# Attention and Fourier mixing on one core: normalisation moved from VectorE to ScalarE in six more batches, and folds dealt in five pieces

## The chip, the core and the metric

The kernel runs on one core of a Trainium2 chip. The metric is the device time of one execution in microseconds (us), as the median of several runs; lower is better. A core has five engines with a queue each: TensorE (PE; its weight loads are listed apart as PEld), VectorE (DVE), ScalarE (ACT), GpSimd (POOL) and SyncE (SP), which here only issues DMAs. [...]

## What is computed

Eight batches, eight heads, 576 tokens, 64 channels per head, all in float32. First comes attention in which each query keeps its 32 largest scores; then, on the 512 joined channels, the real part of a two-dimensional Fourier transform is added, and a normalised two-layer network on top of it.

```python
scores = scale * np.matmul(q, k.transpose(0, 1, 3, 2))
kth = np.partition(scores, -top_k, axis=-1)[..., -top_k:-top_k + 1]
scores = np.where(scores >= kth, scores, -1000000000.0)
attn = np.exp(scores - np.max(scores, axis=-1, keepdims=True))
attn = attn / (np.sum(attn, axis=-1, keepdims=True) + 1e-09)
attn_out = np.matmul(attn, v)                      # (B, H, S, D)
x = attn_out.transpose(0, 2, 1, 3).reshape(B, S, H * D)
u = x + np.real(np.fft.fft(np.fft.fft(x, axis=1), axis=2))
un = (u - u.mean(-1)) / np.sqrt(u.var(-1) + 1e-06)
out = u + np.maximum(un @ w_ch1, 0.0) @ w_ch2
```

## The kernel before

**Tiles and steps.** Two heads make a pair; a batch has four pairs (NPB), the kernel 32. A pair's scores are cut into nine tiles of 128 query rows by 576 keys, so there are 288 tiles (N), 36 per batch (PER_BATCH). The main loop (L1390) makes one step per tile, and a step i works on several tiles at once: it makes the scores of tile i+3, finds the largest values of tiles i and i+1, masks tile i-1, transposes the probabilities of tile i-2, and after the fifth and the ninth tile of a pair multiplies them with the values. Everything is written out by hand in the order of emission (`manual_schedule`, L1169); an engine runs its instructions in that order.

**The chain of a tile.** TensorE multiplies queries and keys (`scores`, L306; sp L368, tail keys sp_t L338), ScalarE copies the result to S (L371, L342, L360). VectorE takes four rounds of the eight largest values (L389) and three of striking them out (L391). GpSimd derives two bounds nt (`bounds`, L398). ScalarE and GpSimd mask the tile (`mask`, L405 and L408), ScalarE takes the exponential with its row sums (`expo`, L414). TensorE transposes the result (tpP, L435), ScalarE copies it to PT (L438), and `attend` (L463) multiplies it with the values into o (L472), in two parts per pair: ch 0 (three token blocks) and ch 1 (two). These parts are called half pairs below. `attended` copies o to xT (L486) and prepares the reciprocals rd of the row sums (L498, L499).

**From the half pair to x.** `to_tokens` (L502) turns xT back with TensorE into the tile tpx (L512) and multiplies each head's 64 columns by its reciprocal into x, which is [tokens, 512 channels] of the batch. Two ways of doing the multiplication are there: `normalise` on VectorE (L516, and L523 for the short block of ch 0), queued at the end of the same step's VectorE work (`late_now`), and `normalise_on_act` on ScalarE (L535, six multiplications of 64 columns for ch 0, four for ch 1), queued for the next step under "act". In the main loop "act" is run after the first fixed piece of TensorE's work and the mask of tile i-1 (L1450 to L1454). The second way is taken in batch 1 alone, but for its last half pair (L541).

tpx and o come from the PSUM pool ps_o, which has one buffer (L122), so a tile of either kind must have been read before the next is written; this holds from batch 1 on. In batch 0 tpx takes one of three other banks. x has two buffers; `to_tokens` of batch b waits, in the written-out order, until the output of batch b-2 has been sent (L1415 to L1421), and half pairs that had to wait follow each other in consecutive steps, save that from step 76 on none goes into the step of an attention product.

**Folds and transforms.** When x of a batch is complete, `fold_ops` (L607) makes sums and differences of it for each parity `par` of the token frequency: first (L627), second (L586), and third(n) for n = 0, 1, 2, which fold the channels (`fold_channels`, L556: n = 0 in L562 and L559, n = 1 in L559, L573 and L574, n = 2 in L559, L581 and L582). n = 0 writes what n = 1 reads; n = 1 writes columns 0 to 255 of the result fg (and takes one column of n = 0's), n = 2 columns 256 to 511. `dft_tokens` (L644) then reads columns 0 to 255 first and 256 to 511 second as weights of TensorE (yp, L663). In batches 1 to 6 the folds run on GpSimd in the steps named by `at(..., "pool0", ...)` (L1309, L1318), ahead of `bounds` (L1495, L1497); in batches 0 and 7 VectorE does them all in one step. The token DFT of a parity is placed at `ft`: steps T0 + 4 and T0 + 7 in batch 1, T0 + 5 and T0 + 11 in batches 2 to 6.

**The rest of TensorE's work.** The network of batch b-1 runs as `units` during batch b: hidden layer hp (L874, evicted by ScalarE L878), second layer cp, cv, cw (L901, L1071). A planner (`fixed_cost`, `level`, `some`, L1351 to L1385) spreads the units over the steps by estimated TensorE costs; the change touches none of these costs.

Of the kernel before, what the change touches and what calls it, by code (L numbers as in the profile page):

```python
# [72 lines left out]
def kernel(  # L73
# [21 lines left out]
    NPB = H // 2  # L95
# [33 lines left out]
    def bank(shape, name, hold=False):  # L129
        n = banks_free.pop(0)  # L130
        t = ps_m.tile(shape, F32, name=name, tag=f"m{n}", bufs=1)
        if not hold:
            banks_free.append(n)
            return t
        return t, lambda: banks_free.append(n)
# [366 lines left out]
    def to_tokens(pair, ch, at_once=True):  # L502

        b, hp = divmod(pair, NPB)
        if b not in x_of:
            x_of[b] = batp.tile([P, 5, DM], F32, name=f"x_{b}", tag="x", bufs=2)
        x = x_of[b]
        xT, rd = xT_of.pop((pair, ch)), rd_of.pop((pair, ch))
        shape, name = [P, 4, P], f"tpx_{pair}_{ch}"
        tp = ps_o.tile(shape, F32, name=name, tag="o") if at_once else bank(shape, name)  # L510
        for n, t in enumerate(CHUNKS[ch]):
            nc.tensor.transpose(tp[0:ROWS[t], n, :], xT[:, P * n:P * n + ROWS[t]], ident)  # L512
        cols = slice(P * hp, P * (hp + 1))

        def normalise():
            nc.vector.tensor_tensor(  # L516
                out=x[:, 2 * ch:2 * ch + 2, cols].rearrange("p t (e d) -> p t e d", e=2),
                in0=tp[:, 0:2, :].rearrange("p t (e d) -> p t e d", e=2),
                in1=rd[:, 0:4].rearrange("p (t e) -> p t e", e=2).to_broadcast([P, 2, 2, D]),
                op=ALU.mult,  # L520
            )
            if ch == 0:
                nc.vector.tensor_tensor(  # L523
                    out=x[0:TAIL, 4, cols].rearrange("p (e d) -> p e d", e=2),
                    in0=tp[0:TAIL, 2, :].rearrange("p (e d) -> p e d", e=2),
                    in1=rd[0:TAIL, 4:6].to_broadcast([TAIL, 2, D]),
                    op=ALU.mult,
                )

        def normalise_on_act():  # L530
            for n, t in enumerate(CHUNKS[ch]):
                r = slice(0, ROWS[t])
                for e in range(2):
                    hd = slice(D * e, D * (e + 1))
                    nc.scalar.mul(  # L535
                        out=x[r, t, cols][:, hd], in_=tp[r, n, hd],
                        mul=rd[r, 2 * n + e:2 * n + e + 1],
                    )


        if b == 1 and (hp, ch) != (NPB - 1, 1):  # L541
            at(now[0] + 1, "act", normalise_on_act)
        else:
            (late_now if at_once else late_next).append(normalise)
        return 0.14 * len(CHUNKS[ch])
# [38 lines left out]
    def fold_halves(eng, s_, z):  # L584
        for cols, op in ((slice(0, Q2), ALU.add), (slice(Q2, DM), ALU.subtract)):
            eng.tensor_tensor(out=z[..., cols], in0=s_[..., 0:Q2], in1=s_[..., Q2:DM], op=op)  # L586
# [20 lines left out]
    def fold_ops(b, par, eng, space="own"):  # L607

        x = x_of[b]

        if space == "hT":
            sp = batp.tile([P, NIT * CW[0]], F32, name=f"fsp_{b}", tag="hT")

        def buf(n, name, cols=DM):
            if space == "hT":
                return sp[:, 2 * DM * n:2 * DM * n + 2 * cols].rearrange("p (s c) -> p s c", s=2)
            pool, tag = (batp, ("fold_s", "fold_d")) if space == "own" else (attp, ("PT0", "PT1"))
            return pool.tile([P, 2, cols], F32, name=f"{name}_{b}_{par}", tag=tag[n % 2], bufs=1)  # L620

        got = folded[b, par] = []

        def first():
            got.append(buf(0, "sd"))
            op = ALU.add if par == 0 else ALU.subtract
            eng.tensor_tensor(out=got[0], in0=x[:, 0:2, :], in1=x[:, 2:4, :], op=op)  # L627

        def second():
            got.append(buf(1, "zw"))  # L630
            fold_halves(eng, got[0], got[1])

        def third(n):
            if n == 0:
                got.append(buf(2, "fg", DM + Q2))
            fold_channels(eng, got[1], got[2][:, :, 0:DM], got[2][:, :, DM:DM + Q2], n)

        def both():
            third(0)
            third(1)  # L640

        return [first, second, both, lambda: third(2)]

    def dft_tokens(b, par):  # L644
        for g2 in range(2):
            half_of_tokens(b, par, g2)
        return 4.3
# [96 lines left out]
    def add_mixed(b, t):  # L744
        rows, x = ROWS[t], x_of[b]
        us = us_of[b, t > 1 and t < 4][0:rows, CHUNKS[CHUNK_OF[t][0]].index(t), :]
        nc.gpsimd.tensor_tensor(out=x[0:rows, t, :], in0=x[0:rows, t, :], in1=us, op=ALU.add)
# [460 lines left out]
    def at(step, where, fn, cost=0.0):  # L1208
        plan.setdefault((step, where), []).append(fn)
        costs[step] = costs.get(step, 0.0) + cost  # L1210
# [75 lines left out]
    for b in range(B):  # L1286
        end = PER_BATCH * (b + 1) - 1
        last = b == B - 1
        first, soon = b == 0, b == 1
        T0 = end + (2 if first else 3 if soon else 4)  # L1290
        if first:

            for op in fold_tails(b, nc.gpsimd):
                at(T0 - 1, "pool", op)

            def folds(b=b):
                for par, space in ((0, "own"), (1, "hT")):
                    for op in fold_ops(b, par, nc.vector, space):
                        op()
            at(T0, "dve", folds)  # L1300
            ft, fc = (T0 + 1, T0 + 1), T0 + 1
        elif soon:

            for n, op in enumerate(fold_tails(b, nc.gpsimd)):
                at(T0 - 2 + n, "pool0", op)
            for par in range(2):
                def folds(par=par, b=b, T0=T0):
                    for n, op in enumerate(fold_ops(b, par, nc.gpsimd)):
                        at(T0 + 1 + 3 * par + min(n, 2), "pool0", op)  # L1309
                at(T0, "begin", folds)  # L1310
            ft, fc = (T0 + 4, T0 + 7), T0 + 8
        elif not last:
            for n, op in enumerate(fold_tails(b, nc.gpsimd)):
                at(T0 - 2 + n, "pool0", op)
            for par in range(2):
                def folds(par=par, b=b, T0=T0):
                    for n, op in enumerate(fold_ops(b, par, nc.gpsimd)):
                        at(T0 + (6 if par else 1) + n, "pool0", op)  # L1318
                at(T0, "begin", folds)
            ft, fc = (T0 + 5, T0 + 11), T0 + 12  # L1320
        else:
            for op in fold_tails(b, nc.gpsimd):
                at(T0 - 1, "pool0", op)

            def folds(b=b):
                for op in fold_ops(b, 0, nc.vector) + fold_ops(b, 1, nc.vector, "PT"):
                    op()
            at(T0, "dve", folds)

            at(T0 + 1, "pe1", lambda: one_unit() + one_unit() if len(queue) > 1 else 0.0)  # L1330
            ft, fc = (T0 + 1, T0 + 3), T0 + 4
        for par in range(2):
            at(ft[par], "pe1", lambda b=b, par=par: dft_tokens(b, par), 4.3)
        for n, t in enumerate((0, 1, 4, 2, 3)):
            quick = first or last
            s = fc + (0 if first else n // 3 if last else n // 2)
            at(s, "pe2", lambda b=b, t=t, q=quick: dft_channels(b, t, q), 1.75)
            if not quick:
                at(s, "pool2", lambda b=b, t=t: add_mixed(b, t))
                at(s + 1, "dve", lambda b=b, t=t: stats(b, t))  # L1340
            at(s + (1 if quick else 2), "pe", lambda b=b, t=t: channels_first(b, t), 0.6)
            if first and t == 4:
                at(s + 1, "pe", lambda: (queue.extend(waiting), waiting.clear()) and 0.0)
        at(s + 1, "begin" if quick else "dve", lambda b=b: rsqrt(b))
        arrivals.append(s + (1 if quick else 2))
        at(arrivals[-1], "units", lambda b=b: (queue if b else waiting).extend(mlp_units(b)))
# [28 lines left out]
    def one_unit():  # L1375
        c, fn, _ = queue.pop(0)
        fn()
        return c
# [11 lines left out]
    while i < N + 4 or plan or queue or sums:  # L1390
# [93 lines left out]
        first, second = top_ops(i, (2, 3)), top_ops(i + 1, (0, 1))  # L1484
# [62 lines left out]
```

## Time and profile before

| what | value |
|---|---|
| median of 3 runs | 1911.16 us (1910.43 to 1911.83) |
| the profiled execution | 1908.21 us, its span 1906.4 us |
| TensorE busy | 1789.7 us |
| VectorE busy | 1584.5 us |
| ScalarE busy | 1210.0 us |
| GpSimd busy | 909.8 us |
| normalise on VectorE, L516 | 57 times, 422 ns each |
| its second part, L523 | 28 times, 273 ns each |
| normalise on ScalarE, L535 | 36 instructions, 28 of them on 128 partitions (330 ns each) and 8 on 64 |
| folds on GpSimd: L627, L586, L559 (254 columns) | 2364, 1277 and 729 ns each |

A profile line of a group gives the line of the kernel, the engine, the operation, what is written and read, the shape and the count. A line of the waits gives who waited for whom, the sum in us, how often and the longest. A line of the timeline gives the start in us from the span's start, the length of the group in us, and in brackets the idle time before it and what ended that. Busy time of TensorE is that of pipelined matmuls whose ends are modelled.

### The profile page before, as it was taken

The page shows a single profiled execution, that of the slowest core. Times are in us where ns is not written, and L with a number is a line of the kernel's source. Part 1 is how long each engine was busy: PE and PEld are TensorE (multiplying, and loading weights), DVE is VectorE, ACT ScalarE, POOL GpSimd, SP SyncE. Part 2 cuts the span into 40 slices and gives each one's busy share as a digit, 9 for nine tenths or more (in the row PEclk, how much of TensorE's full clock was granted, in tenths as well). Part 3 has the DMA queues.
Part 4 walks back from the last instruction along what each step waited for, and adds up shares of the span by engine and source line. Part 5 has one row for each costly group of instructions (what it writes and reads, how often), then busy time and mean ns, then how long its engine had stood idle before and what let it go on. Part 6 is the DMA issues. An engine that isn't in the chain of part 4 may idle for free.

```text
span 1906.4 us, 28799 instructions
## 1 busy us (share of the span) xinstructions
PE 1789.7 (94%) x9200; PEld 1181.4 (62%) x9200; DVE 1584.5 (83%) x3301; ACT 1210.0 (63%) x3078; POOL 909.8 (48%) x1278
## 2 busy tenths in 40 slices
PE   6567799999999999999999999999999999999999
PEld 3344465474666756667567656667567656667677
DVE  8999999999999998889899988988899988872110
ACT  6878657676766767757676667666676667652100
POOL 4768643546635464345534464245534464241022
PEclk7778899999999999999999999999999999999999
DMA  5323002311104111130113101140113102030132
GB/s 165 112 86 108 20 13 57 92 55 25 47 7 130 33 25 47 42 108 27 25 47 101 50 20 53 41 114 22 25 47 100 51 19 57 25 103 6 50 105 75
DMA packets 184342, 111.25 MB, mean 58 GB/s; under 512 B 125952, under 2 KB 174208, under 8 KB 184192
## 3 DMA queue, kind: packets, MB, share of 16 engines
q1 hardware_dynamic: 183408, 109.20, 20.3%
q8 instruction: 74, 1.21, 0.3%
q14 instruction: 76, 0.62, 0.1%
q10 hardware_dynamic: 784, 0.21, 0.0%
HBM read 93.63 MB, written 15.73 MB: 57 GB/s over the span
## 4 chain that ended last, share of the span: by engine, by line
PE 74%; DVE 11%; ACT 6%; POOL 4%; issue 2%; DMA 2%; SPq 0%; POOLq 0%; DVEq 0%; ACTq 0%
PE hp L874 25%; PE cp L901 10%; PE o L472 7%; PE tpP L435 5%; PE sp L368 5%; DVE m L389 5%; PE cw L1071 5%; PE cv L1071 4%; DVE wk L391 4%; PE yp L663 3%; PE cp L940 3%; PE sp_t L338 2%; POOL wk L408 1%; ACT wk L414 1%; ACT wk L405 1%
## 5 line engine op out<-in xcount | busy, mean ns | idle before, releaser
L408 POOL TENSOR_TENSOR wk<-S,wk 128x576 f32<-128x576 f32 x288 | 408.9, 1420 | 730.8 <-ACT wk L405 697.3
L389 DVE MAX8 m<-wk 128x8 f32<-128x576 f32 x864 | 626.7, 750 | 6.1
L874 PE MATMUL hp<-unT,w 128*128 128x256 f32 (+1 forms) x2048 | 540.3, 411 | 2.6 <-ACT unT L792 2.6
L874 PEld LDWEIGHTS hp<-unT,w 128*128 128x128 f32 x2048 | 374.8, 191 | 124.8 <-issue 26.0
L391 DVE MATCH_REPLACE8 wk<-m,wk 128x576 f32<-128x576 f32 x576 | 427.7, 743 | 0.0
L414 ACT ACTIVATE wk<-wk,nt 128x576 f32<-128x576 f32 x288 | 225.0, 781 | 79.0 <-POOL wk L408 78.0
L405 ACT ACTIVATE wk<-S,nt 128x576 f32<-128x576 f32 x288 | 227.0, 788 | 34.1 <-POOL nt L398 32.9
L435 PE MATMUL tpP<-ident,wk 128*128 128x128 f32 x1152 | 183.4, 283 | 68.5 <-ACT wk L414 44.5
L901 PE MATMUL cp<-w,hT 128*128 128x512 f32 x512 | 240.6, 598 | 0.0
L438 ACT COPY PT<-tpP 128x512 f32<-128x512 f32 (+1 forms) x320 | 171.3, 547 | 106.2 <-PE tpP L435 103.8
L435 PEld LDWEIGHTS tpP<-ident,wk 128*128 128x128 f32 x1152 | 140.4, 145 | 143.7 <-ACT wk L414 67.9
L878 ACT ACTIVATE hT<-hp 128x320 f32<-128x320 f32 (+1 forms) x256 | 105.0, 410 | 195.2 <-PE hp L874 193.0
L389 DVE MAX8 m<-S 128x8 f32<-128x576 f32 x288 | 213.9, 743 | 6.8 <-ACT S L342 6.8
L391 DVE MATCH_REPLACE8 wk<-m,S 128x576 f32<-128x576 f32 x288 | 213.8, 742 | 0.0
L472 PE MATMUL o<-PT,v 128*64 128x256 f32 (+3 forms) x1440 | 193.3, 411 | 2.0 <-ACT PT L438 1.9
L371 ACT COPY S<-sp 128x512 f32<-128x512 f32 (+1 forms) x264 | 141.8, 588 | 50.7 <-PE sp L368 50.3
L368 PE MATMUL sp<-kT,qT 64*128 64x512 f32 (+1 forms) x528 | 161.2, 669 | 5.0 <-ACT means L1259 3.3
L472 PEld LDWEIGHTS o<-PT,v 128*64 128x64 f32 x1440 | 110.6, 151 | 72.8 <-issue 15.7
L901 PEld LDWEIGHTS cp<-w,hT 128*128 128x128 f32 x512 | 88.8, 190 | 86.3 <-issue 86.2
L1016 POOL TENSOR_TENSOR hT<-hT 128x512 f32<-128x512 f32 x64 | 81.5, 1276 | 100.1 <-ACT hT L878 88.4
L1071 PE MATMUL cw<-w,hT 128*128 128x256 f32 x448 | 106.7, 383 | 1.9 <-POOL nt L398 1.2
L1071 PEld LDWEIGHTS cw<-w,hT 128*128 128x128 f32 x448 | 81.4, 190 | 19.4 <-issue 5.2
(157 smaller groups left out, 2178.8 us busy)
## 6 DMA issues: line engine op xcount, KB each, us to landing
w<-w_parts SPq DMA_DIRECT2D x82, 512.0 KB, 4.5
space<-in_moe_w_ch_dram SPq DMA_DIRECT2D x32, 512.0 KB, 3.4
nat<-in_q_dram SPq DMA_DIRECT2D x128, 64.0 KB, 2.2
v<-in_v_dram SPq DMA_DIRECT2D x128, 64.0 KB, 2.2
out_dram<-x SPq DMA_DIRECT2D x32, 256.0 KB, 2.1
nat<-in_k_dram SPq DMA_DIRECT2D x124, 64.0 KB, 2.2
w_parts<-w_t SPq DMA_DIRECT2D x8, 512.0 KB, 2.9
w_s<-w_parts SPq DMA_DIRECT2D x8, 512.0 KB, 5.0
```

Of the source, the lines that this page charges most:

```text
L368: nc.tensor.matmul(sp[r], lhsT=qT[hd, q_cols], rhs=kT[hd, :], start=True, stop=True)
L389: ops.append(lambda src=src, m8=m8: nc.vector.max(out=m8, in_=src))
L391: ops.append(lambda src=src, m8=m8: nc.vector.match_replace(w, m8, src, NEG))
L405: nc.scalar.activation(out=w, in_=Ssb[i], func=AF.Relu, scale=-FAR, bias=Nt[i][:, 1:2])
L408: nc.gpsimd.tensor_tensor(out=w, in0=Ssb.pop(i), in1=w, op=ALU.subtract)
L414: nc.scalar.activation(out=w, in_=w, func=AF.Exp, bias=Nt.pop(i)[:, 0:1], accum_out=den_t[pair % 3][:, c:c + 1],)
L435: nc.tensor.transpose(tp[:, c, :], p_sb[:, k0 + P * c:k0 + P * (c + 1)], ident)
L438: nc.scalar.copy(out=pt[:, NF * he:NF * (he + 1), col:col + w], in_=tp[:, :, o:o + w])
L472: nc.tensor.matmul(o[D * e:D * (e + 1), c0:c1], lhsT=vv[:, c, e, :], rhs=pt[:, 2 * NF if c == NF else NF * e + c, c0:c1], start=(c == 0), ...
L874: nc.tensor.matmul(hp[:, 0:w], lhsT=w1[:, dt, P * it:P * (it + 1)], rhs=unT[:, dt, 0:w], start=(dt == 0), stop=(dt == NDT - 1),)
L901: nc.tensor.matmul(cp, lhsT=hT[:, it, P * n:P * (n + 1)], rhs=w2[:, it, :], start=(it == 0), stop=(it == NIT - 1),)
L1071: nc.tensor.matmul(dst, lhsT=h()[a][:, kc, :], rhs=rhs_of(kc), start=start and kc == 0, stop=kc == NK - 1, skip_group_check=True,)
```

## The change

The condition of L541 goes from batch 1 to all batches but the first: in batches 2 to 7, too, ScalarE normalises all half pairs but the last one of each batch, one step later than VectorE did. The four fold pieces per parity become five: third(0) and third(1) are no longer one piece, and the order of the last two is turned, so that the pieces are first, second, third(0), third(2), third(1). In batch 1 they go to the steps 0, 1, 1, 2, 2 after the parity's start (before: first, then second, then third(0), third(1) and third(2) together), in batches 2 to 6 to the steps 0, 1, 2, 2, 3. Batches 0 and 7 fold on VectorE in one step as before, in the new order of pieces.

```diff
-        if b == 1 and (hp, ch) != (NPB - 1, 1):
+        if b and (hp, ch) != (NPB - 1, 1):
             at(now[0] + 1, "act", normalise_on_act)
         else:
             (late_now if at_once else late_next).append(normalise)
@@ fold_ops
-        def both():
-            third(0)
-            third(1)
-
-        return [first, second, both, lambda: third(2)]
+        return [first, second] + [lambda n=n: third(n) for n in (0, 2, 1)]
@@ batch 1
-                        at(T0 + 1 + 3 * par + min(n, 2), "pool0", op)
+                        at(T0 + 1 + 3 * par + (0, 1, 1, 2, 2)[n], "pool0", op)
@@ batches 2 to 6
-                        at(T0 + (6 if par else 1) + n, "pool0", op)
+                        at(T0 + (6 if par else 1) + (0, 1, 2, 2, 3)[n], "pool0", op)
```

## The prediction

> **What bounds the kernel now.** I first read the page for the span and the engines' shares, then a table of busy time by stretches of about one batch, which says where TensorE still has time to give.
>
> ```profile
> span 1906.4 us, 28799 instructions
> PE 1789.7 (94%) x9200; PEld 1181.4 (62%) x9200; DVE 1584.5 (83%) x3301; ACT 1210.0 (63%) x3078; POOL 909.8 (48%) x1278
> ...
> 473.00:688.00 215.00, 206.59 (x1139) 139.64 (x1138) 202.87 (x421) 150.62 (x395) 107.75 (x160) 1.00 0.19 51
> 688.00:902.00 214.00, 208.98 (x1109) 140.07 (x1108) 192.16 (x399) 143.81 (x370) 104.60 (x155) 0.98 0.19 52
> 902.00:1117.00 215.00, 213.32 (x1132) 141.40 (x1131) 192.68 (x401) 144.99 (x372) 104.32 (x155) 1.00 0.19 52
> 1117.00:1332.00 215.00, 213.57 (x1132) 141.33 (x1131) 192.27 (x399) 145.89 (x374) 104.25 (x155) 1.00 0.20 52
> ```
>
> The columns after the length are PE, PEld, DVE, ACT, POOL. From 902 us on TensorE is idle 1.4 to 1.7 us in 215: it sets the time, in an order written out beforehand. VectorE is at 89%, ScalarE at 67%. Whatever makes TensorE wait is added to the end; whatever only lightens VectorE can return at most TensorE's idle time, which over 473 to 1720 us (the two remaining stretches have PE 213.32 of 215 and 171.28 of 173) is 1247 - 1227.1 = 19.9 us.
>
> Next I read the waits of 688 to 902 us for the tile that the moved step empties, tpx.
>
> ```profile
> DVE x L516 <- PE tpx L512: 5.1, 4, 2.3
> PEld tpx L512 <- DVE x L516: 3.7, 1, 3.7
> PE tpx L512 <- DVE x L516: 3.3, 1, 3.3
> ```
>
> The third line is the key: TensorE's next transposes into tpx waited 3.3 us until the normalisation of the previous half pair had read the bank. tpx and the attention output o share the pool ps_o, which has one buffer. So the end of normalise releases TensorE whenever the next user of ps_o follows closely.
>
> **What the skill says.** "PSUM — Partial Sum Buffer", Engine vs sequencer instructions: the queues of ScalarE, VectorE and GpSimd are strict FIFO, and matmuls start in program order. The trace agrees: at 744.24 us the whole TensorE queue stood 3.26 us behind one transpose. "Perfetto Trace Analysis", Optimization Strategy, says that a recurring gap on the saturated engine can mean too little PSUM for the next tile; here that buffer is ps_o. The same page, Optimizing Scalar/DVE Operations, advises moving work to Scalar if DVE is saturated; the table shows TensorE nearer to saturation than VectorE, so the condition is not met after 902 us. "ScalarE: Activation LUTs", Rules for kernel authors, budgets 0.3 us per ACTIVATE plus 0.83 ns per element, 0.35 us for 64; the trace has 0.32 us for one, but back to back they overlap, and that is what I use:
>
> ```profile
> 291.03 0.80 ACT L405 ACTIVATE wk<-S,nt 128x576 f32<-128x576 f32 x1
> 291.71 1.30 ACT L535 ACTIVATE x<-tpx,rd 128x64 f32<-128x64 f32 x6
> ```
>
> Batch 1 already does it: six in 1.30 us, right after the mask (L405); the fours take 0.93 us (316.14 us).
>
> **The moved normalisation, part by part.** It concerns batches 2 to 7, seven half pairs each: 42, of which 24 have ch 0 and 18 ch 1. Off VectorE go 42 x 0.421 (L516) + 24 x 0.273 (L523) = 24.2 us; onto ScalarE come 24 x 1.31 + 18 x 0.93 = 48.2 us. VectorE isn't the bound, so the 24.2 us are worth nothing by themselves.
>
> What counts is when the bank comes free. Before: VectorE normalised in the same step, about 0.4 to 1 us behind the transposes (983.01 to 983.43). After: in step i+1, in ScalarE's queue behind the copies of that step's scores and the mask of tile i. Two kinds of step use ps_o again in step i+1: another transposition, and the attention product. Regularly the next is two or more steps off and nothing waits. But half pairs pile up at the start of a batch: to_tokens waits until batch b-2 is written (L1419), then goes in consecutive steps. There TensorE meets ScalarE. One such step of before:
>
> ```profile
> 979.69 1.13 PE L368 MATMUL sp<-kT,qT 64*128 64x512 f32 x4
> ...
> 980.75 2.42 PE L874 MATMUL hp<-unT,w 128*128 128x320 f32 x8
> 980.91 1.07 ACT L371 COPY S<-sp 128x512 f32<-128x512 f32 x2 [0.67 <-PE sp L368]
> 981.87 0.79 ACT L405 ACTIVATE wk<-S,nt 128x576 f32<-128x576 f32 x1
> ...
> 983.01 0.38 PE L512 MATMUL tpx<-ident,xT 128*128 128x128 f32 x2
> ```
>
> The mask ends at 982.65, six multiplications then at 983.96; the transposes wanted to start at 983.01: 0.95 us late. The mask itself waits for scores that TensorE makes in this step, so a delayed TensorE delays it equally and later stalls keep their size. I did this sum for every place where the order puts a user of ps_o in the very next step (mask end + 1.31 or 0.93 - start now):
> - batch 2: 512.52 + 1.31 - 510.24 = 3.6.
> - batch 3: 739.20 + 1.31 - 738.04 = 2.5; then the mask of 743.99 is 2.5 later, so 743.99 + 2.5 + 0.93 - 744.24 = 3.2 in all (the 3.26 us wait on VectorE goes, but is replaced); then the attention product, 755.70 + 1.31 - 754.43 = 2.6. Together 5.8.
> - batch 4: 0.95; 994.83 + 1.31 - 995.18 = 0.95; the product, 999.63 + 0.93 - 998.88 = 1.7. Together 3.6.
> - batch 5: 1209.39 + 0.93 - 1207.49 = 2.8; the product, 1213.89 + 1.31 - 1213.50 = 1.7. Together 4.5.
> - batch 6: 0.96 + 0.96 + 1.69 = 3.6 (1412.70, 1424.88, 1428.57).
> - batch 7: 1641.24 + 0.93 - 1641.59 = 0.6.
>
> Five others end before TensorE comes: 0. Sum 21.7 us, all on TensorE. Queued behind the multiplications on ScalarE are the query copy (L290), the hidden layer's evictions (L878), the copies of the probabilities (L438) and the exponential (L414). In the ordinary steps these have room, ScalarE being 67% busy; the tightest is the query copy, 1067.85 against its user at 1068.15. In batch 1 one such step shows a stall of 2.41 us (344.63), of which the multiplications ahead of the query copy are 1.3. I take 0.15 us in 10 steps, 1.5 (from 0 to 10, were each 1 us).
>
> **The folds.** In batches 2 to 6 the four steps of a parity held first, second, third(0) with third(1), third(2): 2.4, 2.5, 3.4 and 1.7 us (timeline of GpSimd, 1091.9 to 1111.2). Now they hold first, second, third(0) with third(2), third(1): 2.4, 2.5, 3.2 and 1.9, nearly nothing. GpSimd's total stays, no DMA is moved. But third(1) now comes last, and the token DFT reads its columns first. Batch 1 shows what that means:
>
> ```profile
> 466.50 1.42 POOL L559 TENSOR_TENSOR fg<-zw 128x254 f32<-128x254 f32 x2
> 467.86 1.71 POOL L559 TENSOR_TENSOR fg<-fg 128x128 f32<-128x128 f32 x4
> 469.49 0.12 POOL L573 MEMSET fg<- 128x2 f32 x1
> ...
> 469.68 1.42 POOL L559 TENSOR_TENSOR fg<-zw 128x254 f32<-128x254 f32 x2
> ...
> 469.67 0.59 PE L663 MATMUL yp<-fs,fg 128*64 128x145 f32 x5 [0.82 <-POOL fg L573]
> ```
>
> TensorE starts at the memset of third(1); third(2) (469.68 to 471.35) runs under its matmuls. With the order turned, third(2)'s 1.67 us come ahead of it. GpSimd's chain in these two steps is mask subtraction, fold, nt, mask, without a break, so moving third(0) a step earlier delays nt by as much as it takes from the next step: no gain. Parity 0 costs 1.7 us, parity 1, whose step follows it, 1.3 more: 3.0. Batch 0 folds on VectorE in the same turned order: third(2) there takes 233.32 to 234.22, 0.9 us, and TensorE waits for parity 1 at 239.37: 0.9. In batches 2 to 6 third(2) ended at 1111.21 and TensorE came at 1112.43, so a third(1) longer by 0.2 us is mostly hidden; batch 3 was close (897.58): 0.5 in all. Without the cover each batch could lose 1.7.
>
> **Given back.** Waits of TensorE on the exponential after 500 us (0.34 + 0.91 + 0.44 us at 522.69, 526.74, 549.55) shrink when TensorE is late, with others of the same sort: -3.0 (from 0 to -6).
>
> Sum: 21.7 + 1.5 + 3.0 + 0.9 + 0.5 - 3.0 = 24.6 us. The profiled execution took 1908.21 us (span 1906.4 and 1.8 around it), so 1932.8; it lies 2.95 us under the median of the three timed runs, 1911.16. The forecast for the median is 1911.16 + 24.6 = 1935.8, say 1936.
>
> **Rivals.**
> - The stalls come, but half of them are made up, because TensorE's queue finds later work ready and ScalarE reaches the multiplications sooner than I add up: 21.7/2 + 4.4 - 6 = 9, so 1920. For it: in 473 to 688 TensorE still has 8.4 us idle. Against it: from 902 us only 1.5 us a batch.
> - Faster: VectorE's queue feeds TensorE, and taking 4.0 us a batch off it removes the waits at 744 us (3.3) and on the exponential (1.7) and about a quarter of the rest of the 19.9, while no stall on ps_o appears: about -7, 1904. It decides if ScalarE ends the multiplications before TensorE's next use, that is 1.0 to 3.6 us earlier than I place them. For it: VectorE 94% busy in 473 to 688. Against: the mask stands ahead of them in a strict queue and waits for this step's scores.
> - That the change does less than it says: the fold steps hardly change after batch 1, as shown; that rival is part of the sum.
>
> **Numbers.** About 0.2% (3.8 us) is what a measurement of this kernel can tell from no change. Forecast case 0.78, own range 1924 to 1946 (stalls a quarter smaller, or ordinary steps at 10 us). Half made up 0.12 (0.10 slower, 0.02 the same). Faster 0.10 (0.08 faster, 0.02 the same). Slower 0.88, same 0.04, faster 0.08. The range of 8 in 10 reaches to the half-made-up case: 1919 to 1946.
>
> **What would show it.** TensorE's transposes L512 and products L472 wait on ScalarE's x L535 about eleven times, 1 to 3.6 us each; TensorE's idle time in 902 to 1117 us grows from 1.7 to about 5 us; the DFT at batch 1's folds starts 1.7 us later against the end of third(0). Wrong would be the forecast if L535 ends before those users start, or if stretches from 902 us keep their 215 us.

## The result, and the profile after

The changed kernel takes 1937.29 us (median of 4 runs, 1935.98 to 1938.34) against 1911.49 us before (4 runs): ratio 1.0135, 95% interval 1.0118 to 1.0153, that is 25.8 us or 1.35% slower. 1936 was forecast.

The page of the changed kernel, with the two lines that answer to those of before, and then its table by stretches (PE, PEld, DVE, ACT, POOL, granted clock of TensorE, DMA share, GB/s). The same clock times now hold work that is up to 25 us late, which matters little for the shares. From the folds on, lines of the changed kernel have numbers smaller by four (L874 of before is L870 here); in some of the runs below they are a few larger.

```profile
span 1936.4 us, 28944 instructions
PE 1798.5 (93%) x9200; PEld 1186.0 (61%) x9200; DVE 1567.6 (81%) x3235; ACT 1250.5 (65%) x3294; POOL 909.9 (47%) x1278
```

```profile
473.00:688.00 215.00, 203.48 (x1077) 138.12 (x1077) 191.99 (x393) 152.87 (x417) 102.14 (x150) 0.98 0.19 51
688.00:902.00 214.00, 203.93 (x1084) 136.40 (x1081) 184.21 (x378) 146.44 (x394) 99.88 (x146) 0.98 0.19 51
902.00:1117.00 215.00, 210.32 (x1115) 138.70 (x1115) 185.77 (x382) 149.16 (x402) 103.79 (x154) 1.00 0.19 51
1117.00:1332.00 215.00, 209.36 (x1090) 136.73 (x1091) 184.98 (x380) 148.15 (x396) 98.47 (x152) 0.98 0.19 51
```

VectorE lost work and ScalarE gained it, as the change says: 66 instructions less and 216 more, in busy time 17 us less and 40 us more. The 24.2 and 48.2 of the prediction add up whole durations; neighbours in a queue overlap a little (below, the multiplications start 0.12 us before the mask ends), and busy time counts that once. TensorE's idle time in the quiet stretch from 902 us went from 1.7 to 4.7 us, as forecast (about 5). Two sums explain the whole span: TensorE's idle time rose by 21.2 us (span less busy time: 116.7 to 137.9) and, not foreseen, its busy time by 8.8 us for the same 9200 matmuls; together the 30.0 us between the two profiled executions. These two differ by more than the medians do, because the profiled execution of before lay 3.3 us under its median and that of after 0.9 us over it.

The waits of the changed kernel show where the idle time came from: who waited for whom, the sum in us, how often, the longest.

```profile
PEld tpx L512 <- ACT x L535: 20.8, 11, 4.3
PE tpx L512 <- ACT x L535: 15.1, 9, 3.5
DVE x L516 <- PE tpx L512: 11.3, 7, 3.2
PEld o L472 <- ACT x L535: 8.5, 5, 2.7
PE o L472 <- ACT x L535: 7.1, 4, 2.5
```

The lines of PE are those of its matmuls, which count here; those of PEld, its weight loads, are mostly the same waits once more. TensorE's matmuls waited 13 times for the multiplications on ScalarE, 9 times with the next transposes and 4 times with the attention product: 15.1 + 7.1 = 22.2 us. The wait of 3.3 us on VectorE is gone. The step that the prediction worked through, now (timeline, TensorE and ScalarE):

```profile
994.89 2.42 PE L870 MATMUL hp<-unT,w 128*128 128x320 f32 x8
995.05 1.07 ACT L371 COPY S<-sp 128x512 f32<-128x512 f32 x2 [0.67 <-PE sp L368]
996.01 0.79 ACT L405 ACTIVATE wk<-S,nt 128x576 f32<-128x576 f32 x1
996.68 1.30 ACT L535 ACTIVATE x<-tpx,rd 128x64 f32<-128x64 f32 x6
997.86 0.44 ACT L874 ACTIVATE hT<-hp 128x320 f32<-128x320 f32 x1
998.03 0.20 PEld L512 LDWEIGHTS tpx<-ident,xT 128*128 128x128 f32 x2 [1.23 <-ACT x L535]
998.04 0.44 PE L512 MATMUL tpx<-ident,xT 128*128 128x128 f32 x2 [0.72 <-ACT x L535]
```

Score copies, mask, six multiplications, and only then the transposes, 0.06 us after the last of them.

The busy time is nearly all the clock's. The granted clock of the changed kernel fell to 0.50 for stretches of 3.4 or 6.8 us, most of them at or right after long waits: after the first 230 us 27.2 us in all, against 10.2 in the profile of before. Half of the difference is 8.5 us, of the 8.8. Here are two such stretches, behind the waits of 2.7 us at 1228 us and of 3.5 us at 756 us:

```profile
756.20:759.70 3.50, 3.50 (x9) 2.31 (x9) 3.43 (x8) 0.00 (x0) 2.50 (x7) 0.51 0.00 0
1227.30:1234.10 6.80, 6.01 (x16) 4.30 (x17) 4.23 (x8) 1.17 (x5) 1.55 (x2) 0.50 0.00 0
```

The Trainium skill, "TensorE: Matmul & The Clock Gate", What's actually happening, says that the array's clock is gated to half by default and after an idle window of about 3.4 us, that this window runs freely, and that activity releases the gate. The traces here agree on the half and on the unit of 3.4 us; but waits of 2.2 to 3.5 us, shorter than or about as long as a window, were followed by half clock too (not every one of them: the wait of 2.5 us at 768 us was not).

Batch 1's folds on GpSimd and the token DFT behind them, in the changed kernel:

```profile
467.24 1.41 POOL L559 TENSOR_TENSOR fg<-zw 128x254 f32<-128x254 f32 x2
...
468.86 1.68 POOL L559 TENSOR_TENSOR fg<-fg 128x128 f32<-128x128 f32 x4
470.49 0.10 POOL L573 MEMSET fg<- 128x2 f32 x1
```

```profile
469.37 0.46 PE L659 MATMUL yp<-fs,fg 128*64 128x145 f32 x2 [1.22 <-POOL fg L559]
470.64 0.58 PE L659 MATMUL yp<-fs,fg 128*64 128x145 f32 x5 [0.81 <-POOL fg L573]
```

The piece of 254 columns, third(2), now stands first, and TensorE still starts at the memset of third(1). It waited 1.22 + 0.81 us here, against 0.32 + 0.82 before.

### The profile page after: what moved, and what is told of

Its sections match the earlier page's. It is cut to its first block, busy times and chain, and to the rows that moved or that the text cites. A ratio compares the mean times of both kernels' runs of the same rounds, so it can differ in the third digit from the quotient of the medians.

```text
span 1936.4 us, 28944 instructions
## 1 busy us (share of the span) xinstructions
PE 1798.5 (93%) x9200; PEld 1186.0 (61%) x9200; DVE 1567.6 (81%) x3235; ACT 1250.5 (65%) x3294; POOL 909.9 (47%) x1278
## 4 chain that ended last, share of the span: by engine, by line
PE 74%; DVE 9%; ACT 8%; POOL 4%; issue 2%; DMA 1%; SPq 0%; ACTq 0%; POOLq 0%; DVEq 0%
PE hp L870 24%; PE cp L897 10%; PE o L472 7%; PE tpP L435 5%; PE sp L368 5%; PE cw L1067 5%; PE cv L1067 4%; DVE m L389 4%; PE yp L659 4%; DVE wk L391 4%; PE cp L936 3%; PE sp_t L338 2%; POOL wk L408 2%; ACT wk L405 2%; ACT wk L414 1%
## 5 line engine op out<-in xcount | busy, mean ns | idle before, releaser
L870 PE MATMUL hp<-unT,w 128*128 128x256 f32 (+1 forms) x2048 | 541.7, 411 | 2.1 <-ACT unT L788 2.1
L870 PEld LDWEIGHTS hp<-unT,w 128*128 128x128 f32 x2048 | 375.7, 192 | 124.8 <-issue 27.1
L874 ACT ACTIVATE hT<-hp 128x320 f32<-128x320 f32 (+1 forms) x256 | 105.1, 411 | 183.5 <-PE hp L870 181.2
L1067 PEld LDWEIGHTS cw<-w,hT 128*128 128x128 f32 x448 | 81.4, 190 | 20.4 <-issue 5.8
```

The lines of the kernel that those rows point to most:

```text
L870: nc.tensor.matmul(hp[:, 0:w], lhsT=w1[:, dt, P * it:P * (it + 1)], rhs=unT[:, dt, 0:w], start=(dt == 0), stop=(dt == NDT - 1),)
L1067: nc.tensor.matmul(dst, lhsT=h()[a][:, kc, :], rhs=rhs_of(kc), start=start and kc == 0, stop=kc == NK - 1, skip_group_check=True,)
```

## The experiments

The theory was that the loss is TensorE waiting for the one buffer of ps_o, because the multiplications stand behind the next step's score copies and mask, with the clock as a consequence. Its rivals: the folds carry the loss; the added 48 us load ScalarE wherever they stand; the halved clock is no part of the loss. All ratios are against the kernel before, run on the same chip, whose medians were 1912.64, 1911.67 and 1911.26 us in the three groups of runs below (e1 to e4, e5 to e8, e9 and e10), each group on a chip of its own. A gain or loss in us that follows a ratio is worked out from the ratio; from the medians it can differ by about 1 us.

### e1: the multiplications alone

```diff
-        if b == 1 and (hp, ch) != (NPB - 1, 1):
+        if b and (hp, ch) != (NPB - 1, 1):
```

> The normalisation as in the changed kernel, the folds as before. Bank theory: the loss is TensorE waiting for ps_o because the multiplications stand behind the next step's score copies and mask, plus the TensorE clock halved after the long waits; the changed kernel had 22.3 us of waits on x L535 against 3.3 on x L516 before, so +19.0, and the clock about +5 of the +8.8: 1935, at least 1930; the eleven waits stay with their sizes. Fold theory (rival: the turned folds carry most of the loss): 1918 or less.

Measured: 1937.23 us, ratio 1.0131 (1.0116 to 1.0147). TensorE's waits on x L535 were 15.1 + 7.2 us, at the same 13 places. So the moved normalisation carries practically the whole loss.

### e2: the folds alone

The diff of the change without its first hunk.

> The folds as in the changed kernel, the normalisation as before. Bank theory: TensorE waits about 2 us more at batch 1's token DFT and has two stretches of halved clock there (3.4 us each, so about 3.4 us lost): 1911.5 + 4.5 = 1916, between 1912 and 1919. Fold theory: 1930 or more.

Measured: 1914.18 us, ratio 1.0012 (1.0005 to 1.0018), 2.3 us. The folds are a small loss. In the changed kernel it can't be seen on top of e1 (1.0135 against 1.0131, with intervals wider than 0.12%).

### e3 and e7: the far half pairs, and the close ones

`close` lists the 20 steps of to_tokens in batches 2 to 7 after which ps_o is used in the very next step. e3 sends the 22 other half pairs to ScalarE, e7 the 20 close ones.

```diff
+        close = (84, 125, 126, 127, 165, 166, 167, 168, 202, 203, 204, 206,
+                 237, 238, 239, 240, 274, 275, 276, 278)
-        if b == 1 and (hp, ch) != (NPB - 1, 1):
+        if b and (hp, ch) != (NPB - 1, 1) and now[0] not in close:              # e3
+        if (b == 1 or now[0] in close) and (hp, ch) != (NPB - 1, 1):            # e7
```

> Folds as before; of batches 2 to 7 only the 22 half pairs after which ps_o isn't used in the very next step go to ScalarE, the 20 others stay on VectorE. Bank theory: no wait on x L535, time as before, 1911.5 (1909 to 1914). Load theory (rival: the added work on ScalarE delays its evictions, wherever it stands): about half of the loss of e1, 1922.

> Folds as before; the complement of e3: only the 20 half pairs after which ps_o is used in the very next step go to ScalarE in the next step, the 22 others stay on VectorE. Bank theory: all of e1's loss, 1937 (1934 to 1939). Load theory: about half of it, 1925.

Measured: e3 1912.52 us, ratio 1.0005 (0.9997 to 1.0013); e7 1935.75 us, ratio 1.0128 (1.0114 to 1.0142). About the same number of half pairs, the same instructions on the same engine: one half costs nothing that can be measured, the other everything. The rival of the load on ScalarE falls for these 22; that the close steps aren't simply busier ones, e4 shows. The waits of e7:

```profile
PE tpx L512 <- ACT x L535: 15.4, 9, 3.8
PE o L472 <- ACT x L535: 7.2, 4, 2.5
```

In e3 TensorE's matmuls have no wait on x L535 at all; it still has the one of before on VectorE:

```profile
PE tpx L512 <- DVE x L516: 3.3, 1, 3.3
```

### e4: the same multiplications at the end of their own step

```diff
+        if b > 1 and (hp, ch) != (NPB - 1, 1):
+            at(now[0], "act_end", normalise_on_act)
-        if b == 1 and (hp, ch) != (NPB - 1, 1):
+        elif b == 1 and (hp, ch) != (NPB - 1, 1):
@@ main loop, after run(i, "dve")
+        run(i, "act_end")
```

> Folds as before; in batches 2 to 7 ScalarE does the same multiplications, but at the end of its queue of the same step, ahead of the next step's score copies and mask. Bank theory: the waits on ps_o go, that of 3.3 us on VectorE at 744 us too, with its 6.8 us of halved clock: 1911.5 - 5 = 1906 (1903 to 1911). Load theory: the same 48 us on ScalarE, so as e1, 1930 or more.

Measured: 1916.02 us, ratio 1.0018 (1.0009 to 1.0027). Against e1 the place in the queue is worth 21 us with nothing else changed, which is the theory; but it did not beat the kernel before, and my number was missed by 10 us. The waits say why:

```profile
PE tpx L512 <- ACT x L535: 4.7, 4, 1.8
...
PE o L472 <- ACT x L535: 2.6, 4, 0.7
```

7.3 us remain. ScalarE ends the multiplications 0.3 to 1.8 us after TensorE could have used the bank again, at eight places; VectorE, in the kernel before, kept TensorE waiting at one. At 744 us the wait on VectorE is replaced by two of 1.34 and 1.24 us.

### e5: the folds dealt evenly, in the old order

```diff
-        return [first, second] + [lambda n=n: third(n) for n in (0, 2, 1)]
+        return [first, second] + [lambda n=n: third(n) for n in (0, 1, 2)]
```

This against e2; the normalisation is that of before.

> The normalisation as before; the folds dealt in five pieces to the same steps as in the changed kernel, but in the old order, so that what the token DFT reads first is folded first. Theory that the turned order costs and the dealing doesn't: as the kernel before, ratio 1.000 (0.9992 to 1.0008), and TensorE starts the DFT under the last piece again. Rival, that the dealing costs: 1.0012 as with the folds of the change.

Measured: 1909.09 us, ratio 0.9987 (0.9981 to 0.9994). The even deal by itself is a gain of 2.5 us, which neither side expected; so against e2 the turned order costs 2.3 + 2.5 = 4.8 us. In the other batches these folds stand in the same steps and order as before, so the gain is batch 1's, and it is at parity 1: at parity 0 TensorE waits 0.60 and 0.49 us in e5, against 0.32 and 0.82 before. GpSimd's timeline there, first in e3 (old folds, and the time of the kernel before), then in e5:

```profile
482.75 0.19 POOL L398 TENSOR_TENSOR nt<-m,cc 128x2 f32<-128x2 f32 x1
485.87 1.42 POOL L408 TENSOR_TENSOR wk<-S,wk 128x576 f32<-128x576 f32 x1 [2.94 <-ACT wk L405]
487.23 0.19 POOL L563 COPY fg<-zw 128x4 f32<-128x4 f32 x1
487.38 1.41 POOL L560 TENSOR_TENSOR fg<-zw 128x254 f32<-128x254 f32 x2
488.74 1.69 POOL L560 TENSOR_TENSOR fg<-fg 128x128 f32<-128x128 f32 x4
```

```profile
483.51 1.41 POOL L559 TENSOR_TENSOR fg<-zw 128x254 f32<-128x254 f32 x2
484.88 0.19 POOL L398 TENSOR_TENSOR nt<-m,cc 128x2 f32<-128x2 f32 x1
486.28 1.41 POOL L408 TENSOR_TENSOR wk<-S,wk 128x576 f32<-128x576 f32 x1 [1.21 <-ACT wk L405]
487.64 1.70 POOL L559 TENSOR_TENSOR fg<-fg 128x128 f32<-128x128 f32 x4
```

GpSimd stood idle for 2.94 us before the mask; third(0) now fills 1.6 us of that. TensorE's wait of 1.44 us at the DFT of parity 1 goes (only the 0.82 on the memset stays). The rest of the 2.5 us is likely clock: e3 has a stretch at half clock from 491.5 us, and of the eight profiles with the old folds six have one there; e5 and e10 have none.

### e6: the waits filled with needless work

e1 with 16 transposes of the identity ahead of those of three steps. They go to a spare tile and nothing reads them.

```diff
+        if now[0] in (85, 127, 204):
+            fill = ps_t.tile([P, 4, P], F32, name=f"fill_{now[0]}", tag="tp")
+            for n in range(16):
+                nc.tensor.transpose(fill[:, n % 4, :], ident, ident)
```

> As e1 (multiplications on ScalarE in the next step, old folds), with 16 needless transposes on TensorE ahead of the transposes of steps 85, 127 and 204, where TensorE waited 3.4, 3.5 and 2.7 us; they lie inside the waits and their result isn't read. Clock theory (a part of the loss is TensorE's clock halved after long waits): the halved stretches near these three places go, 13 to 17 us at half clock, so TensorE's busy time falls by 4 to 7 us and the time from 1937 to 1931 (1928 to 1934). Rival (the waits alone are the loss): unchanged, 1936 to 1938.

Measured: 1933.53 us (1931.32 to 1934.47), ratio 1.0116 (1.0100 to 1.0131). More work, and less time: 3.7 us by the medians, 2.9 by the ratios. The runs of e1 (1935.34 to 1938.01) and e6 don't overlap, but they are of different chips, and the intervals of the two ratios do overlap, so the times alone don't settle it; the clock in the traces does for one place. e1 first, then e6, around step 204:

```profile
1223.00:1233.00 10.00, 7.29 (x22) 4.28 (x21) 7.71 (x15) 3.44 (x9) 1.56 (x2) 0.67 0.13 30
```

```profile
1222.00:1232.00 10.00, 9.19 (x50) 6.30 (x49) 7.80 (x15) 5.75 (x18) 1.56 (x2) 1.00 0.14 31
```

The hidden layer's matmuls behind the wait, in e1 and in e6:

```profile
1227.34 0.90 PE L512 MATMUL tpx<-ident,xT 128*128 128x128 f32 x3 [2.71 <-ACT x L535]
1228.03 3.40 PE L874 MATMUL hp<-unT,w 128*128 128x320 f32 x6
```

```profile
1223.65 1.97 PE L512 MATMUL fill<-ident 128*128 128x128 f32 x16
1226.43 0.55 PE L516 MATMUL tpx<-ident,xT 128*128 128x128 f32 x3 [0.81 <-ACT x L539]
1226.81 2.32 PE L878 MATMUL hp<-unT,w 128*128 128x320 f32 x8
```

With the wait filled, clock and matmuls are at full speed; the changed kernel, e1 and e7, where it isn't filled, have 6.8, 6.8 and 3.4 us at half clock there. At step 127 a stretch only moved to the unfilled wait of step 126. At step 85 e6 has 3.4 us where e1 had 6.8, but the changed kernel and e7 have 3.4 too, so that place tells nothing. In all, half clock after 230 us fell from 27.2 us in e1 to 20.4, which is worth 3.4 us and fits the saving. TensorE's busy time didn't fall by the 4 to 7 us expected (1799.1 and 1799.7): I had left out that the needless transposes are busy time themselves, 7.2 us of it. So the halved clock is a part of the loss, a few us of it; what it is worth at the other places isn't shown.

### e8: VectorE's late normalisation at step 126, earlier

```diff
-            (late_now if at_once else late_next).append(normalise)
+            if now[0] == 126:
+                at(now[0], "dve_first", normalise)
+            else:
+                (late_now if at_once else late_next).append(normalise)
@@ main loop, ahead of this step's top_ops
+        run(i, "dve_first")
```

> The kernel before, but at step 126 alone VectorE normalises at the start of its queue of that step and not at its end. Bank theory: the wait of 3.3 us on x L516 goes and with it a stretch of halved clock, so 1912.6 - 3.3 - 1.7 = 1908 (1906 to 1911). Rival (TensorE isn't the bound there and waits for the next thing): 1911.5 to 1913.

Measured: 1911.98 us, ratio 1.0006 (0.9997 to 1.0014): no gain; the rival was right. The wait on x L516 went, and TensorE met another one eleven us later (timeline of TensorE):

```profile
744.86 0.55 PE L512 MATMUL tpx<-ident,xT 128*128 128x128 f32 x3
...
756.33 0.90 PE L435 MATMUL tpP<-ident,wk 128*128 128x128 f32 x3 [4.35 <-ACT wk L414]
```

Around there TensorE isn't the bound. The exponential waits for a mask on GpSimd, and the same trace shows what stands ahead of that one:

```profile
749.64 0.20 POOL L774 TENSOR_TENSOR t<-gi 128x5 f32<-128x5 f32 x1 [2.69 <-DVE gi L770]
...
753.98 1.40 POOL L408 TENSOR_TENSOR wk<-S,wk 128x576 f32<-128x576 f32 x1
...
755.41 0.78 ACT L414 ACTIVATE wk<-wk,nt 128x576 f32<-128x576 f32 x1 [5.32 <-POOL wk L408]
```

From 749.64 to 754.03 us GpSimd works through sixteen small instructions on t and gi (the reciprocal square roots of the layer normalisation), and the first of them had waited for VectorE. In the profile of before they start at 745.70 and the mask at 750.05, both 3.9 us earlier, and VectorE's work ahead of step 126 was 3.9 us earlier too: the early normalisation moved none of them. Taking these sixteen out of the mask's way wasn't tried.

### e9: the close multiplications done twice

```diff
-                for e in range(2):
+                for e in (0, 1) if b == 1 else (0, 0, 1, 1):
```

On top of e7.

> As e7 (20 close half pairs on ScalarE in the next step), but each of their multiplications is done twice, with the same result. Bank theory: at each place the bank comes free 1.31 us (six) or 0.93 us (four) later, less the slack of the seven places that had some (0.1 to 1.65 us): 8 x 1.31 + 3.7 + 5 x 0.93 + 0.9 = 19.8 us more of waits on x L535, at 18 places; time 1936 + 20 + 0 to 8 for the clock, 1959 (1954 to 1965). Rival (ScalarE has room, the waits found so far have another cause that the multiplications merely coincide with): 1936 to 1942.

Measured: 1977.72 us, ratio 1.0343 (1.0329 to 1.0358), 42 us over e7 where 20 to 28 were expected. The direction is the theory's and no rival's: waits at 18 places, the number forecast, on the same two users of the bank.

```profile
PE tpx L512 <- ACT x L535: 36.5, 13, 5.5
...
PE o L472 <- ACT x L535: 15.9, 5, 4.5
```

52.4 us of waits against 22.6 in e7 is 29.8 more, not 19.8. The size was off because doing it twice took more than twice as long: twelve in 3.42 us against six in 1.30.

```profile
514.94 3.42 ACT L535 ACTIVATE x<-tpx,rd 128x64 f32<-128x64 f32 x12
```

With 2.1 us more per six and 1.4 per four (eight in 2.31 us against four in 0.93), the sum of the expectation would have been near 32. TensorE's busy time rose by another 10.3 us (1799.2 to 1809.5), with 57.9 us at half clock after 230 us against 30.6 in e7: 29.8 + 10.3 is nearly all of the 41 us between the two spans.

### e10: the change without its two faults

The changed kernel with e3's condition and e5's order of pieces.

> The changed kernel with its two faults undone: the 20 close half pairs back on VectorE in their own step, and the five fold pieces in the old order. Bank theory: as e5, ratio 0.9987 (0.998 to 0.9995), since the 22 far half pairs cost nothing on ScalarE. Load theory: above 1.000.

Measured: 1910.09 us, ratio 0.9992 (0.9985 to 0.9998): 1.5 us faster than before, a gain that the interval only just tells from none. It and e5 are the versions that beat both kernels. Their intervals overlap, so the 22 far half pairs on ScalarE are neither a gain nor a loss that these runs can tell.

## Why the prediction was right, point by point

**TensorE sets the time.** Right from 902 us on. At 744 us it was wrong (e8): a wait taken away there comes back as another. It cost the forecast nothing, since that wait was replaced and not credited.

**The stalls on ps_o, 21.7 us net.** Right in mechanism and places, and nearly in size. The 13 stalls measured are those of its list; the "about eleven" among its signs miscounts that list. They come to 22.2 us, less the 3.3 us that went: 18.9. The largest were 3.4, 3.5, 2.7 and 2.5 where 3.6, 3.9, 2.8 and 2.6 stood (the 3.9 is the 3.2 "in all", less the 2.5 of the stall before it, and with the 3.26 us that it replaces). Each came out 0.1 to 0.4 us shorter. In the step shown above two things make that up. I put the start of the multiplications at the mask's end, and they start 0.12 us before it (mask 996.01 + 0.79, multiplications from 996.68). And I reckoned a stall from where the transposes would have started, 2.26 us behind the first hp matmul (980.75 and 983.01 before), while the profile counts idle time from the modelled end of the last hp matmul, 0.16 us later. The delay itself is 998.04 - 994.89 - 2.26 = 0.89 us where 0.95 was forecast; 0.72 of it shows as idle time. The zeros were zeros; there are seven of them and not five, since the order has 20 close half pairs.

**Ordinary steps, 1.5 us.** e3 bounds them for the 22 far half pairs: 0.05% (-0.03 to 0.13), so 1.0 us with an interval that holds zero.

**The folds, 3.0 + 0.9 + 0.5 us.** Half right. The turned order costs 4.8 us (e5 against e2), near my 4.4, but not in its parts. In batch 1 TensorE's waits at the token DFT are 3.1 us longer in e2 than in e5 (4.4 against 1.3), the 3.0 of the sum; the rest goes with 3.4 us more at half clock there. The 0.9 of batch 0 didn't come: there these waits are 0.5 us in e2 and 1.3 in e5. (The sign for batch 1, a DFT that starts 1.7 us later against the end of third(0), can't be read as it stands, since third(0) itself moved a step earlier; in the changed kernel TensorE's waits there grew from 3.4 to 5.1 us.) And "no gain" for dealing the pieces out was wrong: it is worth 2.5 us. The step that failed is "without a break". It holds for parity 0 (0.89 us between nt and mask, which is the mask's own way over ScalarE), not for parity 1: there GpSimd waits longer for ScalarE, 1.33 us in the profile of before, 2.94 in e3's (which has a stretch at half clock just ahead, from 477.8 us, and before hasn't), and a piece dealt into that gap is nearly free. e2's net 2.3 us is what the change has of both.

**Given back, -3.0 us.** Too much. TensorE's waits on the exponential after 240 us fell by 1.0 us (9.2 to 8.2).

**The clock, not in the sum.** This is the step that was missing. Long waits can cost twice: once as idle time and once as matmuls at half speed behind them. Against e3, which takes the time of the kernel before, e1's idle time is 18.6 us longer (137.0 against 118.4) and its busy time 7.8 us (1799.1 against 1791.3); e3 has 13.6 us at half clock after 230 us, e1 27.2. With the terms as measured, 2.8 us less for the stalls, 0.5 less for the ordinary steps, 2.1 less for the folds, 2.0 more for what is not given back and 7.8 more for the clock, the sum of 24.6 would be about 29, near the 30.0 between the two profiled executions. The medians are only 25.8 apart, because the profiled execution of before, from which the sum was worked out, was 3.3 us under its median. So the closeness of 1936 to 1937.3 is in part luck: terms too large, and a fast profile at the start, made up for the missing clock.

**The rivals.** Half made up: no, nothing of the stalls was caught up. Faster because VectorE feeds TensorE: no; ScalarE ends the multiplications where I placed them, and e3 and e10, which take 22 normalisations off VectorE without a stall, gain nothing measurable by it.

## What to carry to other kernels

Before a step is moved from a busy engine to an idler one, look at what it releases and where the step will stand in the new queue: here the same multiplications cost nothing for 22 half pairs and 24 us for 20, only because of who wanted the bank in the next step. The free time of an engine over a batch says nothing on this; the order of three instructions in one step does. And when TensorE is the bound, price a long wait on it at more than its length; whether it is the bound at that place is to be checked first, as e8 shows.

## What the runs showed of the hardware that was not expected

- In the changed kernel and its relatives, waits of TensorE of 2.2 to 3.8 us were often, not always, followed by stretches of 3.4 or 6.8 us at a granted clock of 0.50; 16 transposes in a wait of 2.7 us prevented it at one place. The wait of 2.28 us at 477 to 479 us had such a stretch behind it in e1 and e3, and none in the profiles of before and of the changed kernel.
- The kernel before has such stretches itself, and how many differs between executions of nearly the same program: after 230 us its profile has 10.2 us, e3's 13.6, e8's 17.0. Its times spread from 1908.8 to 1914.4 us in 38 runs of one group. A window that runs freely, as in the page quoted above, would fit this; no run tests it.
- Small multiplications on ScalarE back to back cost 0.22 us each (six in 1.30), and 0.285 each when every second one writes the same place again (twelve in 3.42). Why isn't shown.
